# Splitting the first token block of a fused attention and expert kernel around the second

## The chip, the cores and the metric

The kernel runs on one core of a Trainium2 chip. The metric is the device time of one execution in microseconds (us). Five engines work side by side: TensorE (PE) does matmuls, and its weight loads are listed as a sixth row, PEld; VectorE (DVE), ScalarE (ACT) and GpSimd (POOL) do elementwise work; SyncE (SP) issues the DMAs. Matmul results land in PSUM, in eight banks of 128 x 512 fp32; everything else lives in SBUF.

## The reference

Two computations follow each other. The first is linear attention over 8 batches, 8 heads, 576 tokens and 64 channels, with a feature map of 2 x 128 features:

```
proj = x @ w_phi                       # 64 -> 128
proj = proj - max(abs(proj))
phi  = [exp(proj), exp(-proj)]
kv   = phi(k).T @ v ;  z = sum(phi(k))
out  = phi(q) @ kv / (phi(q) . z + 1e-6)
```

Its output, laid out as 4608 tokens of 512 channels, goes through two dense layers, 512 to 2048 to 512, with a leaky ReLU of slope 0.01 between them:

```
h = x @ w_in ;  g = maximum(0.01 * h, h) ;  out = g @ w_out
```

All of it is fp32.

## The kernel before

**Two streams.** Attention is a Python generator that works head pair by head pair (four pairs make a batch, 32 in all). For each pair a k phase makes the small matrix kv and a q phase makes the output of 576 tokens, which is written to the tile `ring`. `ring` holds two batches: batch b goes to half b mod 2. The dense layers, called the expert part here, take the tokens in 18 blocks of 256. The order in which both are written down is made by the main loop; the order in which they run on each engine is chosen when the program is built, by a scheduler that takes the ready instruction of the lowest priority number. First come the loads and the k and q phases of batch 0, then attention (from -500,000 up), then the preparation of the weights (from -250,000), then the expert part (from 0). So the expert part fills what the others leave free, but once the order is fixed each engine keeps to it.

**Precision.** fp32 operands of the dense layers are split into a high part and a low remainder, both of the type fp32r, and a product is three matmuls: high x high, high x low, low x high. This holds for the weights (tiles `w0h`, `w0l`, `w1h`, `w1l`), for the tokens (`xh`, `xl`) and for the hidden values (`gh`, `gl`).

**Weights.** `load_weights` fetches w_in and w_out in 16 parts each. A part is 128 of the 2048 hidden channels. Each part passes through two ACT, several DVE and two split instructions. Its raw data is staged in `ring[:, 1, 2:4]` (w_in), which is batch 1's place for its last two head pairs, and in the buffer `qh` (w_out).

**The expert part.** `split(i)` makes `xh` (ACT) and `xl` (POOL) from `ring` for the 256 tokens of block i; both exist once, so a split waits until the last first-layer matmul of the block before has read them, and of course until attention has written those tokens. A group is a pair (block i, part ft). `layer1(i, ft)` does twelve matmuls of 128 x 256 into a bank `h` (L590, L591, L593), a leaky ReLU in place (ACT, L596), the cast to `gh` (ACT, L68) and the remainder `gl` (DVE, L598). `layer2(i, ft)` does three matmuls of 128 x 512 for each of the two halves of 128 tokens into the two banks `acc` (L609 to L611); these accumulate over the 16 parts, from `start=ft == 0` on. After the last part each half is copied to the tile `o` (one on ACT, one on DVE) and sent to HBM. `layer2` runs `LAG` = 3 groups behind `layer1`. There are two `acc` banks in all, so only one block accumulates at a time.

**Pace.** After each group the loop calls `advance(...)`, which writes down more of the attention stream; before a split it makes sure that the batches which the block needs are written down. Blocks do not align with batches (576 = 2.25 x 256): blocks 0 and 1 lie within batch 0; block 2 takes the last 64 tokens of batch 0 and the first 192 of batch 1; block 4 reaches into batch 2, and block 6 into batch 3. Batch 0's q phases are done in the order tokens 0 to 255, 256 to 511, 512 to 575 for all heads.

**Buffers.** `st(shape, type, tag)` gives a buffer of a tag's slots; tags have one slot unless BUFS says otherwise. The tag `ks` has one slot of 2 x 576 fp32r per partition and is used by the k phases of head pairs from 12 on.

The functions that the diff touches:

Of the kernel before, what the change touches and what calls it, by code (L numbers as in the profile page):

```python
# [9 lines left out]
F32 = mybir.dt.float32  # L10
# [4 lines left out]
ALU = mybir.AluOpType  # L15
AX = mybir.AxisListType

P = 128
B, H, S, D = 8, 8, 576, 64
NP = H // 2  # L20
F = 128
U = 288
DM = 512
DFF = 2048
NFT = DFF // P
T = 256
TT = T // P
NTOK = B * S
NBLK = NTOK // T
LAG = 3  # L30
NN = 8
NK = 8
NF = 12
# [12 lines left out]
def attention_moe_kernel(ctx: ExitStack, tc: tile.TileContext, q, k, v, vt, w_phi, w_in, w_out, out):  # L46
    nc = tc.nc
# [4 lines left out]
    def ct(shape, dt, name):  # L52
        return cp.tile(shape, dt, tag=name, name=name)

    def st(shape, dt, tag):
        return sp.tile(shape, dt, tag=tag, name=tag, bufs=BUFS.get(tag, 1))
# [3 lines left out]
    def pick(key):  # L60
        n = cnt[key] = cnt.get(key, -1) + 1
        e = ENG.get(key, "")
        return e[n % len(e)] if e else None

    def copy_(key, o, i):
        e = pick(key) or "a"
        if e == "a":
            nc.scalar.copy(o, i)  # L68
        else:
            (nc.vector if e == "v" else nc.gpsimd).tensor_copy(o, i)  # L70

    def tt_(key, o, a, b, op):
        (nc.vector if pick(key) == "v" else nc.gpsimd).tensor_tensor(o, a, b, op=op)  # L73

    def pt(tag):
        return ps.tile([P, 512], F32, tag=tag, name=tag, bufs=PBUFS[tag])
# [5 lines left out]
    def weight(which, part, ft):  # L82
        g, f = divmod(ft, 4)
        if (which, part, g) not in weights:
            name = f"w{which}{part}{g}"
            weights[which, part, g] = (cp.tile([P, 4, DM], F32R, tag="late", name=name, bufs=4) if g == 3 else
                                       ct([P, 4, DM], F32R, name))
        return weights[which, part, g][:, f]
# [53 lines left out]
    for j in range(2):  # L142
        r = slice(64 * j, 64 * j + 64)
# [46 lines left out]
    def k_phase(i):  # L190
# [87 lines left out]
        for j in range(2):  # L278
            for t in range(2):
                nc.tensor.transpose(kvtv[:, j, t], kvs[:, j, t], ident[0:66, 0:66])  # L280
        if i < NN:
            kvh = st([P, 2, 2, P], F32, "kvh")
# [276 lines left out]
    def attention():  # L559
        for i in range(NP, B * NP + 1):  # L560
            gens = [k_phase(i)] if i < B * NP else []
            if i > NP:
                gens.append((token_q_phase if i - 1 < NN else q_phase)(i - 1))
            while gens:
# [7 lines left out]
    accs = {}  # L572
    gs = {}

    def split(i):
        for d in range(NP):
            t0 = 0
            while t0 < T:
                c = (i * T + t0) % (2 * S)
                n = min(T - t0, S - c % S)  # L580
                x = ring[:, c // S, d, c % S : c % S + n]
                t1 = t0 + n
                copy_("xh", xh[:, d, t0:t1], x)
                tt_("xl", xl[:, d, t0:t1], x, xh[:, d, t0:t1].bitcast(F32), ALU.subtract)
                t0 = t1

    def layer1(i, ft):
        ph = pt("h")[:, 0:T]
        for d in range(NP):
            nc.tensor.matmul(ph, lhsT=weight(0, "h", ft)[:, d * P : d * P + P], rhs=xh[:, d], start=d == 0, stop=False)  # L590
            nc.tensor.matmul(ph, lhsT=weight(0, "l", ft)[:, d * P : d * P + P], rhs=xh[:, d], start=False, stop=False)  # L591
        for d in range(NP):
            nc.tensor.matmul(ph, lhsT=weight(0, "h", ft)[:, d * P : d * P + P], rhs=xl[:, d], start=False, stop=d == NP - 1)  # L593
        gh = st([P, T], F32R, "gh")
        gl = st([P, T], F32R, "gl")
        nc.scalar.activation(ph, ph, AF.Prelu, alpha=0.01)  # L596
        copy_("gh", gh, ph)
        nc.vector.tensor_tensor(gl, ph, gh.bitcast(F32), op=ALU.subtract)  # L598
        gs[i, ft] = (gh, gl)

    def layer2(i, ft, half=range(TT)):
        if (i, 0) not in accs:
            for t in range(TT):
                accs[i, t] = pt("acc")
        gh, gl = gs[i, ft]
        for t in half:
            ts = slice(t * P, t * P + P)
            a = accs[i, t]
            nc.tensor.matmul(a, lhsT=gh[:, ts], rhs=weight(1, "h", ft), start=ft == 0, stop=False)  # L609
            nc.tensor.matmul(a, lhsT=gh[:, ts], rhs=weight(1, "l", ft), start=False, stop=False)  # L610
            nc.tensor.matmul(a, lhsT=gl[:, ts], rhs=weight(1, "h", ft), start=False, stop=ft == NFT - 1)  # L611
        if ft == NFT - 1:
            for t in half:
                o = st([P, DM], F32, "ek" if i == NBLK - 1 and t else "o")
                copy_("o", o, accs[i, t])
                r = i * T + t * P
                nc.sync.dma_start(out[r : r + P, :], o)

    stream = attention()
    state = {"p": PA, "n": NP - 1}  # L620
# [1 line left out]
    def advance(goal):  # L622
        keep = tc.cur_priority
        tc.cur_priority = state["p"]
        while state["n"] < goal:
            state["n"] = max(state["n"], next(stream, B * NP))
        state["p"] = tc.cur_priority
        tc.cur_priority = keep

    def room(i):  # L630
        return min(B, 2 + i * T // S) * NP
# [12 lines left out]
    tc.cur_priority = PW  # L644
    load_weights()
    tc.cur_priority = 0
    steps = [(i, ft) for i in range(NBLK) for ft in range(NFT)]
    split(0)
    for n, (i, ft) in enumerate(steps):
        layer1(i, ft)  # L650
        advance(min(room(i + 1), NP * (1 + (i + (ft + 1) / NFT) * T / S) + 2))
        if ft == NFT - 1 and i + 1 < NBLK:
            advance(math.ceil((i + 2) * T / S) * NP)
            split(i + 1)
        if n >= LAG:
            layer2(*steps[n - LAG])
    for t in range(TT):
        for s in steps[-LAG:]:
            layer2(*s, [t])
# [36 lines left out]
```

## Time and profile before

| what | us |
| --- | --- |
| median of 3 runs | 1200.2 (1199.45 to 1200.44) |
| profiled execution | 1198.47 |
| its span, first to last instruction | 1196.7 |
| PE busy in it | 1165.8 |
| weight loads busy | 1041.0 |
| ACT busy | 835.0 |
| DVE busy | 759.5 |
| POOL busy | 417.7 |

The profile is one execution. An engine's busy time is the union of its instructions' times. A line such as "L593 PE MATMUL h<-xl,w0h 128*128 128x256 f32 x1152 | 198.6, 282 | 0.6 <-POOL xl L73 0.6" reads: kernel line, engine, operation, written tile <- read tiles, shape, count; then busy us and mean ns of one; then the engine's idle time just before them and what ended most of it. L68, L70 and L73 are the lines of helpers that copy or subtract for many tiles, so the tile names tell what is meant. Digit strings show the busy share in tenths in 40 equal slices of the span, some 30 us each.

### The profile page before, as it was taken

Reading aid. Unit: us, or ns where it says so; the run is one execution under the profiler, and the core shown is the slowest. Engines: PE = TensorE matmul, PEld = TensorE weight load, DVE = VectorE, ACT = ScalarE, POOL = GpSimd, SP = SyncE. Lnnn points to the kernel's source line nnn. Section 1 sums busy time; section 2 is a strip of 40 time slices with the busy share of each in tenths; the row PEclk is TensorE's granted clock in tenths of the full one; section 3 lists DMA queues with packets and bytes.
Section 4 is the critical chain, followed back from the end, with each engine's and each line's share of the span. In section 5 each row is a group of like instructions: output and inputs, shape, how many; then the busy total and the mean of one; then the engine's idle time right before and its main releaser. Section 6 shows DMA issues by size and latency. Waiting matters only on the chain.

```text
span 1196.7 us, 21180 instructions
## 1 busy us (share of the span) xinstructions
PE 1165.8 (97%) x7576; PEld 1041.0 (87%) x7576; DVE 759.5 (63%) x1508; ACT 835.0 (70%) x2104; POOL 417.7 (35%) x418
## 2 busy tenths in 40 slices
PE   8898999999999999999999999999999999999998
PEld 5577788889898989989999999998999999988987
DVE  5998974565777777677777777726777776111111
ACT  5887875676767788888888888837787877432222
POOL 0110011253535364544545455514454544110000
PEclk9999999999999999999999999999999999999999
DMA  7334521111101111011111111101111100000000
GB/s 209 106 116 148 158 86 43 42 49 32 48 22 41 41 35 46 11 49 32 50 31 50 32 50 32 39 22 32 29 50 31 50 1 19 1 19 19 1 19 18
DMA packets 62778, 57.01 MB, mean 48 GB/s; under 512 B 45136, under 2 KB 46288, under 8 KB 62672
## 3 DMA queue, kind: packets, MB, share of 16 engines
q1 hardware_dynamic: 62672, 55.65, 16.1%
q8 instruction: 60, 0.98, 0.3%
q14 instruction: 46, 0.38, 0.1%
HBM read 46.20 MB, written 9.44 MB: 46 GB/s over the span
## 4 chain that ended last, share of the span: by engine, by line
PE 83%; DVE 7%; ACT 4%; issue 2%; DMA 2%; POOL 1%; SPq 0%; DVEq 0%; ACTq 0%
PE h L590 10%; PE h L591 10%; PE h L593 10%; PE acc L609 10%; PE acc L610 10%; PE acc L611 10%; PE c L210 7%; PE a L409 2%; PE a L412 2%; PE a L410 2%; PE a L301 2%; PE a L230 2%; DMA qh<-in_w_out_dram 1%; PE a L328 1%; PE a L369 1%
## 5 line engine op out<-in xcount | busy, mean ns | idle before, releaser
L590 PE MATMUL h<-xh,w0h 128*128 128x256 f32 x1152 | 294.5, 285 | 5.1 <-DVE gl L598 3.4
L591 PE MATMUL h<-xh,w0l 128*128 128x256 f32 x1152 | 291.5, 283 | 1.4 <-DVE w0l L73 1.4
L598 DVE TENSOR_TENSOR gl<-h,gh 128x256 fp32r<-128x256 f32 x288 | 119.5, 418 | 244.5 <-ACT gh L68 230.9
L609 PE MATMUL acc<-w1h,gh 128*128 128x512 f32 x576 | 230.1, 400 | 3.1 <-ACT gh L68 3.0
L590 PEld LDWEIGHTS h<-xh,w0h 128*128 128x128 f32 x1152 | 218.0, 189 | 16.8 <-DVE gl L598 6.0
L610 PE MATMUL acc<-w1l,gh 128*128 128x512 f32 x576 | 228.0, 396 | 0.0
L591 PEld LDWEIGHTS h<-xh,w0l 128*128 128x128 f32 x1152 | 217.8, 189 | 8.6 <-DVE w0l L73 1.6
L596 ACT ACTIVATE h<-h 128x256 f32<-128x256 f32 x288 | 105.8, 369 | 158.4 <-PE h L593 155.4
L611 PE MATMUL acc<-w1h,gl 128*128 128x512 f32 x576 | 202.6, 396 | 0.0
L593 PE MATMUL h<-xl,w0h 128*128 128x256 f32 x1152 | 198.6, 282 | 0.6 <-POOL xl L73 0.6
L73 POOL TENSOR_TENSOR ql<-eq,qh 128x576 fp32r<-128x576 f32 x96 | 145.1, 1526 | 97.9 <-ACT qh L68 85.2
L593 PEld LDWEIGHTS h<-xl,w0h 128*128 128x128 f32 x1152 | 163.6, 189 | 1.6 <-POOL xl L73 0.9
L73 POOL TENSOR_TENSOR kpl<-ek,kph 128x512 fp32r<-128x512 f32 x72 | 96.7, 1343 | 138.3 <-ACT kph L68 71.1
L609 PEld LDWEIGHTS acc<-w1h,gh 128*128 128x128 f32 x576 | 108.5, 188 | 24.2 <-ACT gh L68 4.7
L68 ACT CAST gh<-h 128x256 fp32r<-128x256 f32 x288 | 105.6, 372 | 30.3 <-PE acc L610 25.9
L73 POOL TENSOR_TENSOR ring<-ring,mb 128x576 f32<-128x576 f32 (+2 forms) x45 | 50.7, 1127 | 213.6 <-DVE mb L548 50.3
L610 PEld LDWEIGHTS acc<-w1l,gh 128*128 128x128 f32 x576 | 108.6, 189 | 18.1
L73 POOL TENSOR_TENSOR xl<-ring,xh 128x256 fp32r<-128x256 f32 (+3 forms) x96 | 62.1, 679 | 150.8 <-PE h L593 129.4
L611 PEld LDWEIGHTS acc<-w1h,gl 128*128 128x128 f32 x576 | 98.9, 189 | 8.5
L248 ACT ACTIVATE ek<-pmk 128x256 f32<-128x256 f32 (+1 forms) x128 | 53.3, 417 | 33.6 <-POOL kpl L73 15.9
L210 PE MATMUL c<-kph,vh 128*66 128x256 f32 x240 | 62.4, 282 | 1.8 <-ACT kph L68 1.8
L198 DVE TENSOR_TENSOR ks<-rk,ks 64x576 fp32r<-64x576 f32 x40 | 43.1, 1078 | 30.6 <-ACT ks L68 29.8
(201 smaller groups left out, 2254.6 us busy)
## 6 DMA issues: line engine op xcount, KB each, us to landing
out_dram<-o SPq DMA_DIRECT2D x35, 256.0 KB, 2.1
rk<-in_k_dram SPq DMA_DIRECT2D x29, 288.0 KB, 2.8
ring<-in_w_in_dram SPq DMA_DIRECT2D x16, 512.0 KB, 3.4
qh<-in_w_out_dram SPq DMA_DIRECT2D x16, 512.0 KB, 3.5
rq<-in_q_dram SPq DMA_DIRECT2D x28, 288.0 KB, 3.0
rv<-in_v_dram SPq DMA_DIRECT2D x29, 256.0 KB, 3.4
rv<-in_vt_dram SPq DMA_DIRECT2D x58, 32.0 KB, 2.9
fr<-in_k_dram SPq DMA_DIRECT2D x2, 288.0 KB, 3.3
```

The source lines that it names most:

```text
L68: nc.scalar.copy(o, i)
L73: (nc.vector if pick(key) == "v" else nc.gpsimd).tensor_tensor(o, a, b, op=op)
L210: nc.tensor.matmul(kvp[0 : lt.shape[1], 256 * j : 256 * j + 256], lhsT=lt, rhs=rt, start=first and j == 0, stop=last, skip_group_check=True)
L248: nc.scalar.activation(ek[r, :, 0:F], pmk[r, 2 * s : 2 * s + 2], AF.Exp)
L590: nc.tensor.matmul(ph, lhsT=weight(0, "h", ft)[:, d * P : d * P + P], rhs=xh[:, d], start=d == 0, stop=False)
L591: nc.tensor.matmul(ph, lhsT=weight(0, "l", ft)[:, d * P : d * P + P], rhs=xh[:, d], start=False, stop=False)
L593: nc.tensor.matmul(ph, lhsT=weight(0, "h", ft)[:, d * P : d * P + P], rhs=xl[:, d], start=False, stop=d == NP - 1)
L596: nc.scalar.activation(ph, ph, AF.Prelu, alpha=0.01)
L598: nc.vector.tensor_tensor(gl, ph, gh.bitcast(F32), op=ALU.subtract)
L609: nc.tensor.matmul(a, lhsT=gh[:, ts], rhs=weight(1, "h", ft), start=ft == 0, stop=False)
L610: nc.tensor.matmul(a, lhsT=gh[:, ts], rhs=weight(1, "l", ft), start=False, stop=False)
L611: nc.tensor.matmul(a, lhsT=gl[:, ts], rhs=weight(1, "h", ft), start=False, stop=ft == NFT - 1)
```

## The change

Block 0's parts no longer run in one go. The order of groups becomes: block 0 with parts 0 to 7, block 1 with all 16 parts, block 0 with parts 8 to 15, and then blocks 2 to 17 as before. Since there are two `acc` banks only, block 0's sums over parts 0 to 7 are copied from PSUM to an SBUF tile `held`, in the buffer of the tag `ks`, by the same pair of engines that copied block 0's outputs before. After parts 8 to 15 DVE adds `held` to the second sums as it writes the output tile. `xh` and `xl` exist once, so block 0 is split a second time before its second part; there are 19 splits in place of 18, and the accumulation groups start at parts 0 and 8 of block 0. The calls of `advance` now go by the number n of the step in place of the block's number, so the attention stream is written down at the same steps as before.

```
+CUT = 8
...
+    held = {}
+
     def layer2(i, ft, half=range(TT)):
-        if (i, 0) not in accs:
+        first, last = (ft in (0, CUT), ft in (CUT - 1, NFT - 1)) if i == 0 else (ft == 0, ft == NFT - 1)
+        if first and half[0] == 0:
             for t in range(TT):
                 accs[i, t] = pt("acc")
...
+        if not last:
+            return
+        for t in half:
+            if ft == CUT - 1:
+                if t == 0:
+                    held[0] = st([P, TT, DM], F32, "ks")
+                copy_("o", held[0][:, t], accs[i, t])
+                continue
+            o = st([P, DM], F32, "ek" if i == NBLK - 1 and t else "o")
+            if i == 0:
+                nc.vector.tensor_tensor(o, accs[i, t], held[0][:, t], op=ALU.add)
+            else:
                 copy_("o", o, accs[i, t])
-                r = i * T + t * P
-                nc.sync.dma_start(out[r : r + P, :], o)
+            r = i * T + t * P
+            nc.sync.dma_start(out[r : r + P, :], o)
...
-    steps = [(i, ft) for i in range(NBLK) for ft in range(NFT)]
+    steps = [(i, ft) for i in range(2, NBLK) for ft in range(NFT)]
+    steps = [(0, ft) for ft in range(CUT)] + [(1, ft) for ft in range(NFT)] + [(0, ft) for ft in range(CUT, NFT)] + steps
     split(0)
     for n, (i, ft) in enumerate(steps):
         layer1(i, ft)
-        advance(min(room(i + 1), NP * (1 + (i + (ft + 1) / NFT) * T / S) + 2))
-        if ft == NFT - 1 and i + 1 < NBLK:
-            advance(math.ceil((i + 2) * T / S) * NP)
-            split(i + 1)
+        advance(min(room(n // NFT + 1), NP * (1 + (n + 1) / NFT * T / S) + 2))
+        if n + 1 < len(steps) and steps[n + 1][0] != i:
+            advance(math.ceil((steps[n + 1][0] + 1) * T / S) * NP)
+            split(steps[n + 1][0])
         if n >= LAG:
             layer2(*steps[n - LAG])
```

More of the change, by code (lines that the diff above doesn't have):

```diff
@@ L608, in layer2 @@
             a = accs[i, t]
-            nc.tensor.matmul(a, lhsT=gh[:, ts], rhs=weight(1, "h", ft), start=ft == 0, stop=False)
+            nc.tensor.matmul(a, lhsT=gh[:, ts], rhs=weight(1, "h", ft), start=first, stop=False)
             nc.tensor.matmul(a, lhsT=gh[:, ts], rhs=weight(1, "l", ft), start=False, stop=False)
[L611 to L614, printed above, removed]
+            nc.tensor.matmul(a, lhsT=gl[:, ts], rhs=weight(1, "h", ft), start=False, stop=last)
+        if not last:
[10 more added lines that the diff above has]
+            else:
                 copy_("o", o, accs[i, t])
-                r = i * T + t * P
-                nc.sync.dma_start(out[r : r + P, :], o)
+            r = i * T + t * P
+            nc.sync.dma_start(out[r : r + P, :], o)
     stream = attention()
```

## The prediction

> **What bounds the kernel now.** I read the busy shares first, then the stretches of time, then the split of the token block, which is where the two halves of the kernel meet.
>
> ```profile
> span 1196.7 us, 21180 instructions
> PE 1165.8 (97%) x7576; PEld 1041.0 (87%) x7576; DVE 759.5 (63%) x1508; ACT 835.0 (70%) x2104; POOL 417.7 (35%) x418
> PEld 5577788889898989989999999998999999988987
> DVE  5998974565777777677777777726777776111111
> PE 83%; DVE 7%; ACT 4%; issue 2%; DMA 2%; POOL 1%; SPq 0%; DVEq 0%; ACTq 0%
> L593 PE MATMUL h<-xl,w0h 128*128 128x256 f32 x1152 | 198.6, 282 | 0.6 <-POOL xl L73 0.6
> L596 ACT ACTIVATE h<-h 128x256 f32<-128x256 f32 x288 | 105.8, 369 | 158.4 <-PE h L593 155.4
> L68 ACT CAST gh<-h 128x256 fp32r<-128x256 f32 x288 | 105.6, 372 | 30.3 <-PE acc L610 25.9
> L598 DVE TENSOR_TENSOR gl<-h,gh 128x256 fp32r<-128x256 f32 x288 | 119.5, 418 | 244.5 <-ACT gh L68 230.9
> ```
>
> TensorE (PE) is the bound: 83% of the chain that ended last is PE. A matmul's row runs on to its modelled end, so 97% says little about how tightly matmuls follow each other; the weight loads (PEld) show that better, and they are thin at the start. By stretches (length, then busy time and count of PE, PEld, DVE, ACT, POOL; then the granted PE clock, the DMA share, GB/s):
>
> ```profile
> 100.00:175.00 75.00, 70.60 (x392) 55.92 (x391) 67.08 (x139) 62.29 (x149) 8.36 (x13) 0.98 0.44 128
> 175.00:243.00 68.00, 68.00 (x416) 58.57 (x414) 33.25 (x71) 38.44 (x104) 14.11 (x19) 1.00 0.17 48
> 437.00:502.00 65.00, 63.75 (x440) 58.70 (x440) 48.35 (x98) 53.51 (x139) 31.70 (x29) 1.00 0.14 37
> 502.00:695.00 193.00, 192.90 (x1327) 177.47 (x1326) 145.71 (x286) 158.88 (x399) 100.17 (x93) 1.00 0.14 38
> 1050.00:1190.00 140.00, 136.99 (x868) 123.18 (x867) 22.19 (x51) 39.79 (x112) 8.75 (x16) 1.00 0.03 12
> ```
>
> From 502 to 695 us the loads fill 177.47/193 = 0.92 of the time; from 100 to 175 only 55.92/75 = 0.746. The early stretch thus holds (0.92 x 75 - 55.92)/0.92 = 14.2 us of PE time that is not used. The Trainium skill (Perfetto Trace Analysis, Identifying the Most-Contended Engine) likewise judges PE by its weight loads and not by matmul busy time; by the latter the room would be 75 - 70.60 = 4.4 us, and the rows agree with the page, since 392 matmuls in 75 us is 5.2 per us against 1327/193 = 6.9.
>
> The cause is the preparation of the weights, which block 0 follows group by group:
>
> ```profile
> L68 ACT CAST w0h<-ql x16: 597/618/627, 27.8 to 159.9; 128x512 fp32r<-128x512 f32 x16
> L73 DVE TENSOR_TENSOR w1l<-ql,w1h x16: 640/685/1260, 33.9 to 165.7; 128x512 fp32r<-128x512 f32 x16
> L68 ACT COPY o<-acc x18: 572/587/595, 174.1 to 1192.3; 128x512 f32<-128x512 f32 x18
> L70 DVE COPY o<-acc x17: 651/691/694, 177.3 to 1151.1; 128x512 f32<-128x512 f32 x17
> ```
>
> Sixteen groups' weights come ready one per (159.9 - 27.8)/15 = 8.8 us, the last at 166.4, and block 0 is evicted at 174.1. A group costs PE much less: the last stretch above is expert work alone, 868/18 = 48 groups in 140 us, 2.9 us each. From 175 to 243 block 1 shares PE with attention and takes 68/16 = 4.25 us a group.
>
> **Where the two halves meet.** A block's split needs two things: that the block before has finished reading xh and xl, and that attention has written the tokens. The POOL rows tell which came last (start, duration; ring is a head pair's finished output, xl the split):
>
> ```profile
> 97.35 0.73 POOL L73 TENSOR_TENSOR ring<-ring,mb 128x256 f32<-128x256 f32 x1 [8.12 <-ACT ql L159]
> 217.69 0.75 POOL L73 TENSOR_TENSOR ring<-ring,mb 128x256 f32<-128x256 f32 x1
> 243.04 4.45 POOL L73 TENSOR_TENSOR xl<-ring,xh 128x64 fp32r<-128x64 f32 x8 [0.90 <-PE h L593]
> 369.31 1.44 POOL L73 TENSOR_TENSOR ring<-ring,mb 128x576 f32<-128x576 f32 x1 [4.39 <-DVE mb L421]
> 376.22 4.43 POOL L73 TENSOR_TENSOR xl<-ring,xh 128x128 fp32r<-128x128 f32 x8 [3.05 <-ACT xh L68]
> 500.99 1.44 POOL L73 TENSOR_TENSOR ring<-ring,mb 128x576 f32<-128x576 f32 x1 [3.67 <-ACT gh L68]
> 502.38 3.92 POOL L73 TENSOR_TENSOR xl<-ring,xh 128x192 fp32r<-128x192 f32 x8
> ```
>
> Block 2 needs batch 1's last head pair, tokens 0 to 191: ready at 218.4, used at 243.0, 24.6 us to spare. Block 4 needs all of batch 2: ready at 370.75, used at 376.2, 5.5 us to spare. Block 6 needs all of batch 3: ready at 502.43, and the split starts as it ends. So at block 6 the experts have caught up with attention, and an earlier start of theirs buys only what attention gives.
>
> **The change part by part.**
>
> *Groups moved.* Block 1's tokens are ready at 98.1 (the row at 97.35), about when group 7's weights are (27.8 + 7 x 8.8 = 89, and w_out's after it). From there block 1's groups 0 to 7 have their weights. Eight would cost 8 x 2.9 = 23 us of PE; the room is 14.2 us, or 4.9 groups. I take five groups as the lead at 175 us; the ends are none and eight. At 4.25 us a group that is 21 us of elapsed time by which the later blocks could start earlier (ends 0 and 34).
>
> *ACT and DVE for them.* Five groups need 5 x (0.369 + 0.372) = 3.7 us of ACT and 5 x 0.418 = 2.1 of DVE. From 100 to 175 ACT has 75 - 62.29 = 12.7 us free and DVE 75 - 67.08 = 7.9. That idle time hides them. Without that cover they push back weight preparation and attention, by 0 to 5.8 us. I take 0, since the experts' instructions stand behind both in priority.
>
> *The lead meets attention.* With 21 us in hand block 2 would be asked for at 243 - 21 = 222, after 218.4: no wait. Block 4 would be asked for at 355 and its tokens come at 370.75: a wait of 15.5 us. Block 6 then waits for the remaining 5.5. If attention keeps its pace, all 21 us are waited away and the gain is 0. What remains is how much faster attention runs while the experts wait. The experts' part of ACT and DVE from 437 to 502 is the row of the tile h (PE, PEld, DVE, ACT):
>
> ```profile
> 437.00:502.00 65.00, 27.08 (x192) 24.96 (x192) 6.49 (x16) 11.91 (x33) 1.00 0.14 37
> ```
>
> Without it ACT's work falls from 53.51 to 41.60 (a pace 1.29 times as fast if ACT set it), DVE's from 48.35 to 41.86 (1.155). No row shows attention alone with a full load, so the speed-up lies between 1.0 and 1.29, and I take 1.2, between the two engines. Waiting X and gained 0.2X make up 21: X = 17.5, gain 3.5 us (ends 0 and 21 x 0.29/1.29 = 4.7).
>
> *A third switch of block.* split(0) is done twice; the second adds four casts and four POOL subtractions:
>
> ```profile
> L68 ACT CAST xh<-ring x96: 238/372/421, 51.8 to 1142.6; 128x256 fp32r<-128x256 f32 x48, 128x64 fp32r<-128x64 f32 x16, 128x192 fp32r<-128x192 f32 x16, 128x128 fp32r<-128x128 f32 x16
> L73 POOL TENSOR_TENSOR xl<-ring,xh x96: 314/734/1249, 52.3 to 1144.6; 128x256 fp32r<-128x256 f32 x48, 128x64 fp32r<-128x64 f32 x16, 128x192 fp32r<-128x192 f32 x16, 128x128 fp32r<-128x128 f32 x16
> ```
>
> That is 4 x 0.372 = 1.5 us of ACT and 4 x 0.734 = 2.9 of POOL. Behind POOL's wait for the last reader of xl stands attention's own POOL work. PE itself waited 0.6 us for xl in the whole run (the L593 row), because the three lagging groups' second layer runs meanwhile. Cost 0 to 4.4 us; I take 0.5, near the 0.6 that all seventeen switches show together.
>
> *Held sums.* Two evictions to the held tile take the place of block 0's old ones (0.587 on ACT, 0.691 on DVE), and they do not wait for an output buffer. The two later DVE adds are not in the trace; the nearest row, the DVE eviction of the same tile from PSUM, is 0.691. Below by nothing, above by twice that for the second operand: 1.3 to 2.8 us of new work, at about 210 us where DVE is busy 33.25 of 68. The second add waits on DVE for the first output's DMA, as the copy at 177.3 does, with gl behind it. I take 0.3 on the path (0 to 2.8). The buffer is that of ks:
>
> ```profile
> L68 ACT CAST ks<-rk x40: 658/672/679, 311.1 to 964.3; 64x576 fp32r<-64x576 f32 x40
> ```
>
> Its first use is at 311, some 95 us after the adds. The two output DMAs move behind block 1's on SP; nothing reads them.
>
> *Clock.* The granted clock fell once as PE thinned out:
>
> ```profile
> 90.00:95.00 5.00, 4.00 (x24) 3.24 (x24) 4.12 (x9) 2.99 (x7) 0.00 (x0) 1.00 0.56 157
> 95.00:100.00 5.00, 5.00 (x31) 4.80 (x31) 4.93 (x11) 4.21 (x10) 0.73 (x1) 0.68 0.48 161
> 115.00:120.00 5.00, 3.87 (x12) 3.19 (x13) 2.88 (x6) 4.36 (x13) 0.00 (x0) 0.73 0.72 213
> ```
>
> At 0.68 and 0.73 of full, two such dips take 5 x 0.32 + 5 x 0.27 = 3.0 us of PE speed. More work may remove the second (-1.4 to 0); I take -0.3. The Trainium skill (TensorE: Matmul & The Clock Gate, Part 1) says that an idle window of some 3.4 us halves the clock. The rows agree, and it speaks against this change: in the 17.5 us in which the experts would wait, attention alone keeps PE sparse, and it would then run its matmuls at half speed. My sum leaves that out.
>
> Sum: -3.5 + 0.5 + 0.3 - 0.3 = -3.0 us. After 502 us PE is filled to the end, so the shift is carried through. The profiled execution took 1198.47 us, 1.8 over its span; the median of the runs is 1200.2, so I forecast 1197.2.
>
> **The rivals.** (A) *The room is won whole.* Attention is slowed by standing behind expert matmuls in PE's queue, not by its own chain; then fewer of them let it run ahead. For it: PE is 83% of the chain. Against it: attention is ahead of the experts in priority. Time: -14.2 + 0.8, about 1187.
> (B) *Slower: attention pushed back from 100 to 175.* DVE is busy 67.08 of 75 there and works in order; eight groups (8 x 0.741 + 8 x 0.418 = 9.3 us of ACT and DVE) stand between attention's steps. If half falls on its chain and waiting gives nothing back, batch 3 ends 4.6 us later, and with the switch 0.5: 1205. It decides from the point where batch 3's last multiplication ends after 502.4. Against it: the 7.9 us still free on DVE.
> (C) *No change.* Attention's pace is its own latency; all 21 us are waited away at blocks 4 and 6: 1200.2, up to 1 us more.
> (D) *It does not do what it says.* Lowest in priority, block 1's groups find no slot before the weights end; the lead is nothing and the switch costs 1: 1201.
>
> **How the numbers follow.** Forecast 0.36 (own range 1194.5 to 1199.7), A 0.17, B 0.20, C 0.21, D 0.06. A change under 0.2% (2.4 us) can't be told from none. Faster: A and most of the forecast with a little of C, 0.45; same 0.33; slower: B and some of D, 0.22. The range takes in A's and B's ends: 1187 to 1207.
>
> **What would show it.** Right: more than 392 matmuls between 100 and 175 us; block 2's split near 222; a thin PE ahead of block 4's split, waiting for batch 2's last multiplication; batch 3's at about 499. A is right if that one comes before 492, B if after 503, C if between, D if block 2 is still split at 240. My forecast is wrong if attention's pace between 220 and 500 does not move with the experts' waiting, or moves much more.

## The result: slower by 0.9%

The changed kernel takes 1210.8 us (median of 6, 1208.8 to 1212.9); the kernel before takes 1199.8 beside it. The ratio is 1.0091 with a 95% interval of 1.0078 to 1.0104, which is 11 us. The forecast was 1197.2, with a range up to 1207. The profiled execution is the longest of the six (1212.93, span 1211.1), so what follows accounts for 14.4 us between two profiles, a little more than the medians differ.

The head of the page after:

```profile
span 1211.1 us, 21189 instructions
PE 1173.1 (97%) x7576; PEld 1044.9 (86%) x7576; DVE 767.2 (63%) x1510; ACT 835.1 (69%) x2108; POOL 415.3 (34%) x422
PE 86%; DVE 6%; ACT 4%; issue 2%; DMA 1%; POOL 1%; SPq 0%; DVEq 0%; POOLq 0%; ACTq 0%
```

The work is the same: 7576 matmuls, two more DVE instructions, four more of ACT and of POOL. It is spread over more time. To see where, I cut both executions at the first matmul of block 2, block 6, block 11 and block 17 (length of the stretch, then busy time and count of PE, PEld, DVE, ACT, POOL, then clock, DMA share, GB/s). Before:

```profile
56.10:245.90 189.80, 181.31 (x1041) 150.84 (x1042) 144.44 (x299) 140.49 (x343) 32.31 (x47) 0.98 0.33 97
245.90:505.20 259.30, 254.38 (x1721) 232.01 (x1720) 178.81 (x344) 196.31 (x502) 121.85 (x113) 1.00 0.13 36
505.20:811.90 306.70, 306.60 (x2106) 282.23 (x2105) 215.24 (x420) 241.82 (x611) 147.99 (x134) 1.00 0.14 38
811.90:1144.50 332.60, 329.60 (x2202) 301.42 (x2201) 171.70 (x350) 203.97 (x531) 110.57 (x109) 1.00 0.08 23
```

After:

```profile
57.30:221.60 164.30, 159.69 (x932) 133.52 (x933) 125.76 (x256) 121.75 (x299) 25.16 (x40) 1.00 0.35 103
221.60:510.20 288.60, 277.46 (x1835) 250.95 (x1833) 198.66 (x390) 216.40 (x551) 128.00 (x124) 0.98 0.13 38
510.20:826.50 316.30, 311.64 (x2104) 284.10 (x2103) 221.93 (x418) 240.79 (x611) 146.72 (x134) 0.99 0.13 37
826.50:1158.90 332.40, 329.30 (x2201) 301.16 (x2200) 171.50 (x350) 203.82 (x531) 110.46 (x109) 1.00 0.07 23
```

The experts do get their lead: block 2 begins 24.3 us earlier. All of it is gone by block 6, which begins 5.0 us later than before. From block 6 to block 11 another 9.6 us are lost on the same 2100 matmuls. From block 11 on the two run alike to 0.2 us.

**Where the lead went.** POOL's rows of the changed kernel at the points shown in the prediction (ring is attention's output, xl the split):

```profile
190.82 0.32 POOL L74 TENSOR_TENSOR ring<-ring,mb 128x64 f32<-128x64 f32 x1 [7.65 <-DVE mb L338]
218.91 2.84 POOL L74 TENSOR_TENSOR xl<-ring,xh 128x64 fp32r<-128x64 f32 x7 [1.73 <-ACT xh L69]
233.62 0.73 POOL L74 TENSOR_TENSOR ring<-ring,mb 128x256 f32<-128x256 f32 x1
234.81 0.59 POOL L74 TENSOR_TENSOR xl<-ring,xh 128x192 fp32r<-128x192 f32 x1 [0.46 <-ACT xh L69]
366.12 2.99 POOL L74 TENSOR_TENSOR xl<-ring,xh 128x128 fp32r<-128x128 f32 x7
380.90 1.41 POOL L74 TENSOR_TENSOR ring<-ring,mb 128x576 f32<-128x576 f32 x1 [5.51 <-PE c L211]
385.42 0.79 POOL L74 TENSOR_TENSOR xl<-ring,xh 128x128 fp32r<-128x128 f32 x1
506.78 1.44 POOL L74 TENSOR_TENSOR ring<-ring,mb 128x576 f32<-128x576 f32 x1
```

Batch 1's last head pair, which was ready for block 2 at 218.4, is ready at 234.35: attention is 15.9 us late. Seven of block 2's eight split pieces are done by 221.7 and the last one waits for it until 234.8. At block 4 the same happens again, 369.1 to 385.4: batch 2 is ready there at 382.3, 11.6 us late. Attention then makes up some ground, and batch 3, ready at 502.43 before, is ready at 508.2, 5.8 us late. That is where the 5.0 us at block 6 come from.

**Why attention is late.** The last multiplication of head pair 5 is a fixed point in attention. In the kernel before, POOL's timeline has it at 175.16:

```profile
175.16 0.32 POOL L73 TENSOR_TENSOR ring<-ring,mb 128x64 f32<-128x64 f32 x1 [6.85 <-DVE mb L337]
```

The stretch up to that point, with the instructions on the tile h alone (PE, PEld, DVE, ACT); PE did 340:

```profile
0.00:175.50 175.50, 64.37 (x340) 46.87 (x340) 7.45 (x18) 21.36 (x56) 0.98 0.46 137
```

In the changed kernel the point comes at 190.82, and the same view has there:

```profile
0.00:191.10 191.10, 77.11 (x436) 58.51 (x436) 10.66 (x26) 27.54 (x73) 1.00 0.43 127
```

That is 96 matmuls more, or 8 groups of 12. So eight more groups run on PE before the same step of attention. At 2.9 us each they take 23 us; 15.7 of these delay attention, and only some 7 fill time that PE had free. The chain of waits from 108 to 180 us in the changed kernel, by line, holds nothing but PE:

```profile
by line: PE c L211 16.5%; PE h L591 10.5%; PE a L329 10.4%; PE acc L615 10.2%; PE h L594 10.2%; PE a L302 10.1%; PE h L592 10.0%; PE acc L613 9.7%; PE acc L614 9.3%; PE a L320 2.8%; PE c L281 0.7%
```

**The second loss.** Who waited longest from block 6 to block 11? In the kernel before, the view of PE's waits from 505 to 826 us is empty. In the changed kernel it reads (who, line, for whom: total us, times, longest):

```profile
PE c L211 <- ACT kph L69: 1.5, 1, 1.5
PE h L591 <- DVE gl L599: 1.3, 3, 0.5
PE h L594 <- POOL xl L74: 0.8, 1, 0.8
PE acc L613 <- ACT o L69: 0.6, 1, 0.6
PE a L413 <- POOL ql L74: 0.2, 1, 0.2
```

These are several unrelated causes, each small. They sum to 4.4 us, about PE's idle time in the stretch (316.30 - 311.64 = 4.7). The rest of the 9.6 us stands as longer busy time, and part of it is the clock, which falls for a few us behind the first of these waits (the clock is the third number from the end):

```profile
515.00:520.00 5.00, 3.32 (x18) 2.34 (x17) 4.76 (x14) 4.41 (x14) 1.84 (x2) 0.88 0.56 164
520.00:525.00 5.00, 5.00 (x28) 4.64 (x27) 3.32 (x6) 2.88 (x8) 3.26 (x2) 0.78 0.14 52
```

That is 0.12 + 0.22 of 5 us each, 1.7 us. Some 3 us are left that these views do not divide. In the traces PE's matmuls stand in the same order in both kernels up to number 460 of 7576, differ from there on, and stand in one order again for the last 2613, where the times agree too. The experiments ask whether this loss comes from the change or from the new order as such.

### The profile page after: what moved, and what is told of

Read it like the earlier page. It is cut to its first block, busy times and chain, and to the rows that moved or that the text cites. A ratio compares the mean times of both kernels' runs of the same rounds, so it can differ in the third digit from the quotient of the medians.

```text
span 1211.1 us, 21189 instructions
## 1 busy us (share of the span) xinstructions
PE 1173.1 (97%) x7576; PEld 1044.9 (86%) x7576; DVE 767.2 (63%) x1510; ACT 835.1 (69%) x2108; POOL 415.3 (34%) x422
## 4 chain that ended last, share of the span: by engine, by line
PE 86%; DVE 6%; ACT 4%; issue 2%; DMA 1%; POOL 1%; SPq 0%; DVEq 0%; POOLq 0%; ACTq 0%
PE h L591 11%; PE h L592 11%; PE acc L613 10%; PE h L594 10%; PE acc L615 10%; PE acc L614 10%; PE c L211 7%; PE a L302 2%; PE a L413 2%; PE a L410 2%; PE a L411 2%; PE a L231 2%; PE a L329 1%; PE a L371 1%; PE a L370 1%
## 5 line engine op out<-in xcount | busy, mean ns | idle before, releaser
L199 DVE TENSOR_TENSOR ks<-rk,ks 64x576 fp32r<-64x576 f32 x40 | 45.7, 1142 | 34.7 <-ACT ks L69 33.7
```

## The experiments

I call the theories Q (in PE's fixed order the extra groups stand ahead of attention), E (their ACT and DVE work delays it; this is rival B's reason), M (held sums and third split cost it), and for the second loss O (any new order loses there) and S (a real shortage of work behind a late attention). "Slip" below is how much later than 218.4 batch 1's last head pair is ready for block 2. "Blocks 6 to 10" is the time from block 6's first matmul to block 11's, 306.7 us before and 316.3 after.

### Fewer matmuls in the extra groups

```
+        thin = i == 1 and ft < CUT
...
-            nc.tensor.matmul(ph, lhsT=weight(0, "l", ft)[:, d * P : d * P + P], rhs=xh[:, d], start=False, stop=False)
-        for d in range(NP):
+            if not thin:
+                nc.tensor.matmul(ph, lhsT=weight(0, "l", ft)[:, d * P : d * P + P], rhs=xh[:, d], start=False, stop=False)
+        for d in range(0 if thin else NP):
...
+            if i == 1 and ft < CUT:
+                continue
             nc.tensor.matmul(a, lhsT=gh[:, ts], rhs=weight(1, "l", ft), start=False, stop=False)
```

> Leaves out, for block 1's parts 0 to 7, every matmul with a low part (8 of 12 in the first layer, 4 of 6 in the second), so that stretch of the output is less exact; ACT, DVE and the order of groups stay. That takes 8 x (8 x 0.119 + 4 x 0.232) = 15.0 us from PE between 100 and 175 us. Theory Q (queue: in PE's fixed order the eight extra groups stand ahead of batch 1's attention, and PE has no room for them): batch 1's last head pair is ready for block 2 at 219 to 223 (before 218.4, after 234.3). Then the experts have their lead at no cost to attention, and the time shows what such a lead is worth while attention sets the pace up to block 6: 1195 to 1203. Theory E (the extra groups' work on ACT and DVE pushes attention back): still 230 to 236, and 1205 to 1211. Theory M (held sums and third split cost it): attention and time as in the changed kernel.

Measured: 1203.3 us, ratio 1.0026 (1.0015 to 1.0037). The slip falls from 15.9 to 6.4 us, by POOL's timeline:

```profile
224.08 0.73 POOL L74 TENSOR_TENSOR ring<-ring,mb 128x256 f32<-128x256 f32 x1
```

The early stretch of this run (columns as above, PE to POOL):

```profile
100.00:175.00 75.00, 69.28 (x394) 55.03 (x393) 68.78 (x141) 64.07 (x157) 12.23 (x17) 1.00 0.43 130
```

ACT and DVE are no less busy than in the changed kernel (there 61.44 and 66.39), PE does 394 matmuls in place of 437. So most of the slip goes with the matmuls, a little less than Q said (ready at 224.8, expected 219 to 223; the time, too, is just above its range). M, which expected attention as in the changed kernel, is out as the main cause: held sums and third split are both in this run. The 6.4 us that are left can come from the 8 us of the extra groups' matmuls that are still there (8 x 2.9 - 15.0); no run separates them from the third split. Block 2 begins 33 us earlier than before and block 6 only 1.4 us earlier. Even a lead that costs attention 6 us is almost wholly waited away by block 6. Blocks 6 to 10 take 314.1.

### No ACT and DVE work in the extra groups

```
+        if i == 1 and ft < CUT:
+            gs[i, ft] = (xh[:, 0], xl[:, 0])
+            return
         gh = st([P, T], F32R, "gh")
```

> Leaves out, for block 1's parts 0 to 7, the leaky ReLU, the cast to gh and the remainder gl; the second layer multiplies parts of xh and xl instead, so these parts of the output are wrong. All matmuls stay. That takes 8 x (0.369 + 0.372) = 5.9 us from ACT and 8 x 0.418 = 3.3 from DVE between 100 and 175. Theory Q: batch 1's last head pair for block 2 still at 230 to 236, time 1206 to 1212. Theory E: back at 219 to 225, time 1198 to 1204. Theory M: as Q.

Measured: 1205.1 us, ratio 1.0039 (1.0024 to 1.0053). Batch 1's last head pair on POOL's timeline:

```profile
235.42 0.73 POOL L74 TENSOR_TENSOR ring<-ring,mb 128x256 f32<-128x256 f32 x1 [0.78 <-DVE mb L338]
```

and the early stretch of this run:

```profile
100.00:175.00 75.00, 73.11 (x430) 60.53 (x429) 65.44 (x126) 55.48 (x125) 8.62 (x11) 1.00 0.40 121
```

ACT is 6 us less busy, DVE 1 us, and attention is no earlier: 236.2, a slip of 17.8. E falls. The time is a little under Q's 1206, because blocks 6 to 10 take only 310.6 here.

### Four groups ahead in place of eight

```
-CUT = 8
+CUT = 12
```

> Cut at part 12: block 1 comes after block 0's part 11, so four groups are ahead and not eight. Held sums and third split are the same. Theories Q and E: about half the slip, batch 1's last head pair at 222 to 228, time 1202 to 1207. Theory M: 1208 to 1212 as with the cut at 8.

Measured: 1209.5 us, ratio 1.0076 (1.0059 to 1.0093). The slip is not halved: 235.3, that is 16.9. At the fixed point in head pair 5 the tile h has 400 matmuls behind it, 60 more than before, so five groups stand ahead in place of eight; the point itself comes 13.9 us late in place of 15.7. Five groups are 14.5 us, so nearly nothing of them fell into free time. A later cut makes the lead smaller and uses less of the room. Q and E had expected half the slip; slip and time are those of M, so this run by itself speaks for M. The run with fewer matmuls rules M out as the main cause, and Q can account for this run, but only after the fact.

Block 6 begins 8.3 us late here (513.5), more than the 5.0 us with eight groups, though the slip is about the same. The experts wait at block 4 from 364.4 to 388.8 there, and PE runs at half clock for most of that time without a break:

```profile
373.00:393.50 20.50, 14.69 (x59) 12.20 (x58) 14.24 (x30) 12.05 (x30) 7.51 (x8) 0.50 0.26 71
```

Batch 2 is ready at 388.4, 17.7 us late: up to there attention has won nothing back, while in the changed kernel it was 11.6 us late. Blocks 6 to 10 take only 309.7 us.

### Held sums alone

```
-    steps = [(0, ft) for ft in range(CUT)] + [(1, ft) for ft in range(NFT)] + [(0, ft) for ft in range(CUT, NFT)] + steps
+    steps = [(0, ft) for ft in range(NFT)] + [(1, ft) for ft in range(NFT)] + steps
```

> Block 0's sums are held after part 7 and added at the end, but block 1 stays behind block 0, so no group is moved and there is no third split. Theories Q and E: 1199 to 1202, batch 1's last head pair at 217 to 221. Theory M: most of the loss stays, 1206 to 1211.

Measured: 1206.6 us, ratio 1.0057 (1.0042 to 1.0072). By the time this looks like M. By the stretches it is not: attention is 1.4 us early at block 2, block 6 begins 0.3 us early, and everything is lost after it, with 314.0 us for blocks 6 to 10. PE's longest waits there have other causes than in the changed kernel:

```profile
PE a L410 <- ACT qh L69: 1.9, 3, 0.8
PE c L211 <- POOL kpl L74: 1.8, 2, 1.0
```

No theory had expected that. It is the second loss of the changed kernel without any group moved and with attention early, which led to O and S.

### A change that moves nothing early: an ACT cast repeated

```
-                copy_("kh", ks[o, j], rk[o])
+                for _ in range(4 if i == 17 else 1):
+                    copy_("kh", ks[o, j], rk[o])
```

> The kernel before, with the ACT cast of ks in the k phase of head pair 17 done four times and not once (4.0 us of ACT more, on attention alone, which has 61 us to spare from there to block 9). PE's order is the same up to matmul 2641 and in the last 2615; only blocks 6 to 10 are ordered anew. Theory O: 1202 to 1209, all of it lost between block 6's and block 11's start. Theory S: 1199 to 1201.5.

Measured: 1206.6 us, ratio 1.0053 (1.0038 to 1.0068). Blocks 6 to 10 as one stretch:

```profile
505.90:818.80 312.90, 310.05 (x2114) 285.61 (x2113) 219.49 (x427) 242.55 (x614) 147.93 (x139) 0.99 0.13 37
```

and PE's waits in it:

```profile
PE c L211 <- DVE ms L380: 2.5, 1, 2.5
PE h L591 <- DVE gl L599: 0.4, 1, 0.4
```

Up to block 6 it is within 0.7 us of the kernel before. Then 6.2 us are lost, by the number as O said. But the loss has one place, the wait of 2.5 us and half clock behind it (PE's row, and the stretch of 5 us that holds it):

```profile
515.26 0.45 PE L211 MATMUL c<-kph,vh 128*66 128x256 f32 x1 [2.50 <-DVE ms L380]
515.00:520.00 5.00, 4.38 (x17) 3.72 (x18) 4.83 (x14) 2.90 (x8) 1.83 (x2) 0.50 0.39 113
```

From 510 to 525 us the clock is 0.94, 0.50 and 0.88, which makes 3.4 us; with the wait that is nearly the whole loss. The added casts stand on ACT from 491.3 to 501.7, just ahead of it, and attention's matmul at 515.26 runs at 510.69 in the kernel before. So this run does not separate a new order from attention being some 4 us late there. That attention has 61 us to spare before block 9 does not help where PE's order has its step next. For O the run with held sums alone, where attention is early, is better evidence, and so is the next one.

### Output copies with their engines exchanged

```
-"o": "av"
+"o": "va"
```

> The kernel before, with the output copies' engines exchanged (first half on DVE, second on ACT, so no work more or less); the scheduler's order changes from matmul 631 on. Theory O: 1202 to 1212, lost in PE gaps. Theory S: 1199 to 1202.

Measured: 1206.4 us, ratio 1.0052 (1.0037 to 1.0067). Blocks 6 to 10:

```profile
507.20:820.80 313.60, 308.07 (x2094) 281.24 (x2093) 217.91 (x406) 236.15 (x602) 144.19 (x131) 1.00 0.12 35
```

and PE's waits in them:

```profile
PE a L409 <- ACT tq L415: 3.5, 3, 1.6
PE h L590 <- DVE gl L598: 2.0, 4, 1.1
```

No work is added or taken, the clock is 1.00, and 6.9 us go in blocks 6 to 10, by other waits again. O stands and S, which expected 1199 to 1202, falls.

### The change with one and the same order behind block 6

Two tiny copies make attention's first steps after block 6's split wait for it. Kernel before and changed kernel then have the same order on PE for the last 4820 matmuls.

```
             ks = st([P, 2, S], F32R, "ks")
+            if i == 17:
+                nc.vector.tensor_copy(ks[:, 0, 0:1], xl[:, NP - 1, T - 1 : T].bitcast(F32))
...
         qs = st([P, 2, S], F32R, "qs")
+        if i == 16:
+            nc.vector.tensor_copy(qs[:, 0, 0:1], xl[:, NP - 1, T - 1 : T].bitcast(F32))
```

> The kernel before, with one tiny DVE copy at the head of the k phase of head pair 17 and of the q phase of head pair 16 that reads the end of block 6's split: attention cannot start them earlier, in this kernel as in its pair. The order of the last 4820 of PE's 7304 matmuls, from block 6 on, is then the same in both of the pair. Theory O (order: the fixed order of blocks 6 to 10 in the kernel before is packed without a gap of PE; most other orders lose 3 to 9 us there, whatever the cause of the new order): 1202 to 1212. Theory S (shortage: attention is late at block 6, and the experts lack work behind it): 1200 to 1208, the wait alone.

> The changed kernel with the same two copies. Theory O: slower than its pair by what is lost before block 6 alone, 4 to 7 us (5.0 in the profiles without the copies). Theory S: slower than its pair by 9 to 13, as without the copies.

Measured: 1209.4 us (ratio 1.0079, 1.0062 to 1.0096) without the change and 1212.6 us (ratio 1.0105, 1.009 to 1.012) with it. Blocks 6 to 10, first without the change:

```profile
505.60:822.20 316.60, 309.88 (x2112) 283.11 (x2111) 221.79 (x430) 241.61 (x615) 142.81 (x135) 1.00 0.14 38
```

and with it:

```profile
508.80:825.20 316.40, 309.73 (x2111) 282.88 (x2110) 223.31 (x430) 241.55 (x615) 141.97 (x135) 1.00 0.14 38
```

With one order the stretch takes the same time. The whole difference of 3.2 us stands at block 6's start (505.6 and 508.8) and stays until the end. This is a little under the 4 to 7 that O expected and far from S's 9 to 13. Without the copies block 6 begins 5.0 us late, so of the changed kernel's loss 3 to 5 us are the change's own; the rest goes with the order that the kernel before has and this one has not. The copies also hold attention back, so the 9.9 us that they cost the kernel before in this stretch do not tell order from lateness.

### The lead without its price, and the held sums, in that same form

The same two copies in the run with fewer matmuls and in the run with held sums alone.

> The run that leaves out the low-part matmuls of block 1's parts 0 to 7, with the two copies that hold attention at block 6; the last 4820 matmuls then stand on PE as in the held pair. The lead of the experts costs attention little here, so the difference to the held kernel before is what a lead of eight groups is worth if PE had room for it. If attention sets the pace up to block 6: -3 to +1 us against 1209.4, that is 1206 to 1210.5. If PE's total work did, it would be -15 us or more: about 1195.

Measured: 1203.6 us, ratio 1.0028 (1.0018 to 1.0038). That is 5.8 us under the held kernel before by the medians and 3.7 by the profiled spans (1203.2 and 1206.9); block 6 begins 3.2 us earlier. It is more than the 3 expected at most, and far from the 15 us of matmuls left out. Attention's pace takes most of the lead, but not all of it.

> Held sums without moved groups, with the two copies. The order from block 6 on is the held pair's in its last 3383 matmuls only. If the held sums cost nothing by themselves, and the 6.7 us of the run without the copies were the new order of blocks 6 to 10: within 2 us of 1209.4. If they cost something themselves: 1214 or more.

Measured: 1205.3 us, ratio 1.0045 (1.003 to 1.006), some 4 us under the held kernel before, outside both expectations. Block 6 begins 3.0 us earlier and blocks 6 to 10 take 317.2. Held sums cost nothing that can be seen; that M is out was expected, the small gain before block 6 was not.

## Why the prediction was wrong, step by step

**What bounds the kernel.** PE does. The room from 100 to 175 us was put at 14.2 us, by a ceiling of 0.92 for the weight loads. The changed kernel's row of that stretch:

```profile
100.00:175.00 75.00, 73.97 (x437) 61.46 (x436) 66.39 (x134) 61.44 (x146) 8.12 (x11) 1.00 0.41 122
```

and two pieces of its chain of waits from 108 to 180 us (start, length, count of matmuls):

```profile
122.02 0.86 PE a L329 x4
121.08 0.48 PE h L594 x4
```

Only 5.5 us of loads were added before PE was the whole chain, at a share of 0.82 (61.46 of 75). The ceiling came from a stretch with another mix: attention's matmuls here are plain fp32 and take 0.86/4 = 0.215 us for 256 columns, an expert matmul of 256 columns takes 0.12, and both have one weight load. Of the room, 7 us were used, nearer to the 4.4 us by matmul busy time that the prediction set aside.

**Groups moved.** Five groups by 175 us, 21 us of lead: the tile h has 187 matmuls between 100 and 175 us against 132, 4.6 groups more, and block 2 begins 24.3 us earlier. The number is right, the reason is not: the five groups were to fit into free time, and they took attention's turns instead.

**ACT and DVE for them.** The step said that idle time hides the groups, at 0, "since the experts' instructions stand behind both in priority". This is the first step that failed. Priority decides when the order is made; on the chip eight groups stand ahead of attention's next matmul on PE, and PE had time for a third of them. The slip was 15.9 us. Rival B had the place (attention from 100 to 175) and the direction, but the wrong engine (the run without ACT and DVE work shows it) and 4.6 us for the price.

**The lead meets attention.** Block 2's wait was put at none and was 13 us, because of the slip. Block 4's was put at 15.5 us and was 16 us, but that is luck: it was asked for at 369 in place of 355, and batch 2 was ready at 382.3 in place of 370.75. That attention sets the pace up to block 6 held: a lead of 33 us in the run with fewer matmuls left 1.4 us at block 6.

**Attention's speed-up.** Put at 3.5 us, at most 4.7. The slip fell from 15.9 to 5.8 us between 234 and 508 us, so attention won back 10.1, partly while the experts waited. The term was too small. With the true slip the sum up to block 6 is 15.9 - 10.1 = +5.8, in place of -3.5.

**Third switch, held sums.** 0.8 us in all, on the path. For the held sums nothing speaks against it: the adds are at their lower bound,

```profile
L626 DVE TENSOR_TENSOR o<-acc,ks x2: 690/690/691, 225.9 to 228.7; 128x512 f32<-128x512 f32 x2
L71 DVE COPY ks<-acc x1: 680/680/680, 112.6 to 112.6; 128x512 f32<-128x512 f32 x1
```

and the run with held sums alone loses nothing before block 6. The third split was never run alone. From 100 to 235 us of the changed kernel PE waited for POOL's part of a split twice, both times at the switch to block 1 (104 us) and not at block 0's second split:

```profile
PE h L594 <- POOL xl L74: 1.0, 2, 0.5
```

**Clock.** Put at -0.3 us; the half clock during the waiting was named and left out of the sum. Both early dips are gone (1.00 from 57.3 to 221.6). New ones stand where the experts wait for block 4:

```profile
375.00:380.00 5.00, 2.71 (x15) 2.22 (x14) 3.87 (x9) 2.16 (x6) 0.38 (x1) 0.88 0.28 105
380.00:385.00 5.00, 4.11 (x24) 3.01 (x22) 4.91 (x8) 3.40 (x7) 3.23 (x3) 0.77 0.00 2
390.00:395.00 5.00, 5.00 (x31) 4.79 (x31) 4.50 (x9) 4.30 (x11) 1.27 (x1) 0.75 0.00 0
```

The Trainium skill (TensorE: Matmul & The Clock Gate, Part 1) had spoken for that, and these rows agree that the clock falls when PE thins out. They show no idle window of 3.4 us, though: PE's longest wait from 366 to 392 us is 2.1 us. From block 3's start to block 5's the clock is 0.97 over 66.4 us and 0.96 over 79.2 us, which is some 5 us of full clock; with four groups ahead it was 0.50 for 20.5 us. How much of this lies on the path, no run separates.

**"After 502 us PE is filled to the end, so the shift is carried through."** This is the step that failed most: 9.6 us in the profiles. It took the filled PE of the kernel before for a property of the work. It is a property of one order. In the eleven other kernels, which have eight orders there, blocks 6 to 10 take 309.7 to 317.2 us against 306.7, also where no group was moved. No rival had this, so the range missed the time; without it, the change costs 3 to 5 us, and 1203 to 1205 lies inside.

What stays open: why the scheduler puts eight groups of lower priority ahead of attention (its own timing was not set against the chip's), what the half clock costs on the path, and what makes the order of the kernel before fit so well from block 6 on. None of the kernels run beats it.

## What to carry to other kernels

Where each engine follows an order made beforehand, low priority is no cover: price work put into an engine's free time at its full length on whatever stands behind it in that queue, and count as room only what that engine can use with the mix of that stretch. Before a lead is worth anything, find who sets the pace at the next place where the two streams meet; here it was waited away there. And when an edit makes a scheduler order everything anew, run a control that reorders and moves no group: here held sums alone and exchanged engines cost 0.6% and 0.5%, more than the edit's own part. Look where the control's loss lies, too: the repeated cast put its own work just ahead of it.

## What was not expected of the hardware

Nine orders of the same 2100 matmuls differ by 10 us in 307 (306.7 to 317.2), through small waits of PE on DVE, ACT and POOL, at other places in each. Three of the kernels with the two copies ran that stretch in one order within 0.4 us of each other (316.6, 316.4 and 316.2), though they came to it at 505.6, 508.8 and 502.4. The changed kernel and the one with fewer matmuls also share one order there, and differ by 2.2 us (316.3 and 314.1): from 515 to 525 us the former has the clock at 0.88 and 0.78, worth 1.7 us, and the latter at 1.00. So the order set the time of a stretch to one or two tenths of a percent, apart from the clock. And a short wait can be paid twice: 2.5 us of waiting in the run with the repeated cast came with a fall of the clock worth 3.4 us.
